# Out by seven products in all four large blocks, with the combined weights made in the plain blocks

## The chip, the cores and the metric

The kernel runs on one core of a Trainium2 chip. The metric is the time of one execution on the device, in microseconds (us). Five engines work side by side, each through its own queue in order: TensorE (PE) multiplies, VectorE (DVE) and ScalarE (ACT) do elementwise work, GpSimd (POOL) helps with attention, and SyncE (SP) issues the DMAs between DRAM and on-chip memory.

## The reference

```python
# attention, q of 8 batches x 8 heads x 576 x 64; k and v averaged over groups of 8 rows (72 rows left)
scores = (1 / sqrt(64)) * q @ k_p.T
attn   = softmax(scores)
x      = (attn @ v_p) arranged as [4608 tokens, 512]
# then a gated layer
h = x @ w_in                       # w_in 512 x 2048
g = h * clip(h + 3, 0, 6) / 6
out = g @ w_out                    # w_out 2048 x 512
```

The weights arrive in 64-bit floats, the rest in 32-bit.

## The kernel before

The 4608 tokens are done in twelve blocks (`BLOCKS`, 512, 256 and ten of 384 tokens). The first four (0 to 3) are "plain"; the other eight are taken in pairs as four "large blocks" of 768 tokens (`supers`, numbered 0 to 3 here). Attention for a later block is cut into small steps that `Paced` spreads over the matmuls of the current one.

Every operand is kept as a high and a low part in the fp32r format, and each product is three matmuls (high x high, high x low, low x high); the stationary operand is always 128 x 128.

A plain block goes through 16 steps, one for each tile of 128 features (`NF`). Step u does `h` (x by w_in, 12 matmuls into one of two PSUM banks, `psh`), then `relu` on ACT, `gate` on DVE, `hi` (tile `ghi`) on ACT and `lo` (tile `glo`) on DVE; `out` (g by w_out into `pso`) comes two steps later. h(u) can begin when gate(u - 2) has read the bank of the same number. The weights stay in SBUF, in tiles `w_f` of the pools `consts[0]` (f below 8) and `consts[1]`. During blocks 2 and 3, functions in a table `hooks` (block, then step) also prepare the large blocks.

A large block multiplies matrices cut in 2 x 2 blocks with seven block products in place of eight. Its in stage (N1, seven products for each of 8 feature pairs) needs x in seven combinations (`x_ops`, run in the plain block 3 for large block 0) and w_in in seven (three raw, four combined). `sums_of` makes the four combined ones: two sums of a pair of tiles and four mixes on DVE, a rounded copy on ACT, a difference on DVE; tile `wq`, stored to DRAM arrays `wd`. `plain_of` stores the raw blocks (to `wd`, and those of w_out to `w2d`).

The out stage has two forms. `out_plain` (large block 0) multiplies g by w_out directly, 288 matmuls of 512 columns. `out_seven` (1 to 3) does seven products of half width, 504 matmuls of 256 columns, with four combined forms of w_out from the DRAM arrays `w2t`. Those are made once, by `combine`, in the out stage of large block 0, where the weights pass by anyway: sums of 512, mixes of 256 and a difference of 1024 elements on DVE (tiles `tq`, `tg`, `th`), a copy of 1024 on ACT, two stores of 512 KB each.

In the large blocks all weights are read back in pieces of 512 KB (`chunk`) into two rings, `ws0` (wsFalse) and `ws1` (wsTrue). The rings lie where the plain blocks' weights were: `swap` frees `consts[0]` in block 3, and the right side is freed after it.

Up to step 3 of block 1 the order of every engine is written out by hand (`ORDER`). From there a scheduler sets each engine's order when the program is built, from its own estimates; on the chip each engine then keeps to that order and waits on semaphores.

Of the kernel before, what the change touches and what calls it, by code (L numbers as in the profile page):

```python
# [98 lines left out]
def attention_moe_kernel(  # L99
# [833 lines left out]
    def sums_of(i, h):  # L933

        half = slice(h * P, (h + 1) * P)
        t = early_x[-1].tile([P, 2, 4, P], F32, name="wq", bufs=1)
        hi, q = t[:, 0], t[:, 1]
        for r, w in enumerate(pair_of(i)):
            nc.vector.tensor_tensor(  # L939
                out=q[:, 2 * r : 2 * r + 2], in0=w[:, 0, :, half], in1=w[:, 1, :, half], op=ALU.add  # L940
            )
            after_mark()
        for to, a, b, how in ((0, 0, 2, ALU.subtract), (2, 2, 3, ALU.add), (3, 3, 0, ALU.subtract), (1, 1, 3, ALU.subtract)):
            nc.vector.tensor_tensor(out=q[:, to], in0=q[:, a], in1=q[:, b], op=how)
# [18 lines left out]
    def chunks_of(n):  # L963
        if n not in SEVEN:
            plain = [w2_dram[f // 4][:, f % 4].rearrange("p q m c -> p (q m c)") for f in range(NF)]
        else:
            plain = []
            for o in KINDS:
                for m in range(NF // 4):
                    if o in RAW2:  # L970
                        r, q = RAW2[o]
                        plain.append(w2_dram[m][:, r::2, q].rearrange("p k m c -> p k (m c)"))
                    else:
                        plain.append(w2t_dram[m][:, PLACED[o]].rearrange("p k m c -> p (k m c)"))
# [31 lines left out]

    def combine(n, i):

        if i % 2 or not i:
            hi, q = (late[1].tile([P, 2 * DM], F32, name=x, tag="ro", bufs=NREL) for x in ("th", "tq"))  # L1010
        else:
            t = late[1].tile([P, 8 * HALF], F32, name="tg", tag=f"g{i - 2}", bufs=1)
            hi, q = t[:, : 2 * DM], t[:, 2 * DM : 4 * DM]
        hi, q = (x.rearrange("p (a c) -> p a c", a=4) for x in (hi, q))
        for r in range(2):
            w = next_w2(n, 2 * i + r).bitcast(F32)
            nc.vector.tensor_tensor(out=q[:, 2 * r : 2 * r + 2], in0=w[:, :, 0], in1=w[:, :, 1], op=ALU.add)
            after_mark()
        for to, a, b, how in ((3, 3, 1, ALU.subtract), (1, 1, 0, ALU.subtract), (0, 0, 3, ALU.add), (2, 2, 0, ALU.subtract)):
            nc.vector.tensor_tensor(out=q[:, to], in0=q[:, a], in1=q[:, b], op=how)  # L1020
            after_mark()
        nc.scalar.copy(hi.bitcast(F32R), q)
# [544 lines left out]
```

## Time and profile before

| | us |
|---|---|
| median of 3 runs | 894.1 (892.81 to 894.3) |
| the profiled execution, its time | 893.88 |
| its span in the profile | 892.1 |
| the four plain blocks, to the start of large block 0 | 345.6 |
| in stage and out stage of large block 0 | 77.6 and 70.8 |
| of large block 1 | 71.6 and 67.2 |
| of large block 2 | 71.2 and 64.7 |
| of large block 3 | 59.5 and 63.9 |

The stages are cut where PE goes over to matmuls of another line. A row of a stretch has, after its length, the busy time and the number of instructions of each engine, the granted TensorE clock, the share of the DMA engines that is busy and GB/s. A row of the chain is one piece of the sequence of work that ended last, with its start, its length and the count of instructions. A row of the timeline has the start, the length and the instruction, and in square brackets the engine's idle time before it and what ended that. Instructions of one engine that follow each other may overlap a little, so start to start is shorter than the length.

### The profile page before, as it was taken

Reading aid. Unit: us, or ns where it says so; the run is one execution under the profiler, and the core shown is the slowest. Engines: PE = TensorE matmul, PEld = TensorE weight load, DVE = VectorE, ACT = ScalarE, POOL = GpSimd, SP = SyncE. Lnnn points to the kernel's source line nnn. Section 1 sums busy time; section 2 is a strip of 40 time slices with the busy share of each in tenths; the row PEclk is TensorE's granted clock in tenths of the full one; section 3 lists DMA queues with packets and bytes.
Section 4 is the critical chain, followed back from the end, with each engine's and each line's share of the span. In section 5 each row is a group of like instructions: output and inputs, shape, how many; then the busy total and the mean of one; then the engine's idle time right before and its main releaser. Section 6 shows DMA issues by size and latency. Waiting matters only on the chain.

```text
span 892.1 us, 15646 instructions
## 1 busy us (share of the span) xinstructions
PE 869.2 (97%) x5360; PEld 812.3 (91%) x5360; DVE 665.9 (75%) x1340; ACT 553.6 (62%) x1515; POOL 83.6 (9%) x168
## 2 busy tenths in 40 slices
PE   7899999999999999999999999999999999999998
PEld 6788888988989998998888999999999999999998
DVE  6999864567877785869788688897597877466664
ACT  5998766655656655778344688665577746355442
POOL 4100002110211100102000101100100200000000
PEclk9999999999999999999999999999999999999999
DMA  9970205995425234996587968877976777877873
GB/s 294 392 293 1 72 24 192 360 327 167 130 67 160 71 129 135 368 315 225 180 271 239 383 218 295 265 239 236 331 250 213 226 233 240 275 253 238 266 264 132
DMA packets 124654, 200.00 MB, mean 224 GB/s; under 512 B 13216, under 2 KB 81056, under 8 KB 124576
## 3 DMA queue, kind: packets, MB, share of 16 engines
q1 hardware_dynamic: 124432, 199.00, 67.8%
q8 instruction: 43, 0.70, 0.3%
q14 instruction: 35, 0.29, 0.1%
q10 hardware_dynamic: 144, 0.00, 0.0%
HBM read 158.08 MB, written 40.89 MB: 223 GB/s over the span
## 4 chain that ended last, share of the span: by engine, by line
PE 80%; DVE 8%; DMA 5%; ACT 4%; issue 2%; SPq 1%; POOL 0%; DVEq 0%; ACTq 0%; POOLq 0%
PE psx L1134 22%; PE psx L1261 19%; PE pso L872 12%; PE psh L841 12%; PE psx L1188 7%; PE psa L646 3%; PE psa L463 3%; ACT e L472 2%; PE psa L572 1%; DMA raw<-w_in_l 1%; DMA raw<-w_out_l 1%; DMA wd<-wq 1%; DVE vst L383 1%; DMA wsFalse<-wd 1%; DVE wq L939 1%
## 5 line engine op out<-in xcount | busy, mean ns | idle before, releaser
L1134 PE MATMUL psx<-x,wsFalse 128*128 128x384 f32 x768 | 151.8, 341 | 1.7 <-DVE g L1098 0.8
L841 PE MATMUL psh<-xhi,w 128*128 128x384 f32 (+2 forms) x520 | 145.9, 340 | 0.5 <-DVE g L853 0.4
L1134 PEld LDWEIGHTS psx<-x,wsFalse 128*128 128x128 f32 x768 | 133.6, 188 | 3.2 <-ACT c L1107 1.3
L1113 ACT CAST part<-g 128x768 fp32r<-128x768 f32 x100 | 83.3, 836 | 85.0 <-PE psx L1261 65.8
L1115 DVE TENSOR_TENSOR part<-g,part 128x768 fp32r<-128x768 f32 x100 | 95.2, 955 | 46.5 <-ACT part L1113 46.1
L872 PE MATMUL pso<-w,ghi 128*128 128x512 f32 x384 | 120.7, 398 | 0.4 <-ACT o L877 0.4
L1134 PE MATMUL psx<-x,wsTrue 128*128 128x384 f32 x576 | 115.8, 342 | 2.4 <-DMA wsTrue<-wd 2.3
L1261 PE MATMUL psx<-wsFalse,part 128*128 128x256 f32 x864 | 108.3, 282 | 1.5 <-DVE part L1115 1.1
L1261 PEld LDWEIGHTS psx<-wsFalse,part 128*128 128x128 f32 x864 | 105.2, 189 | 2.3 <-DVE part L1115 1.3
L1134 PEld LDWEIGHTS psx<-x,wsTrue 128*128 128x128 f32 x576 | 99.6, 188 | 3.1 <-DVE g L1092 3.1
L841 PEld LDWEIGHTS psh<-xhi,w 128*128 128x128 f32 x520 | 93.2, 188 | 8.2 <-DVE g L853 1.1
L472 ACT ACTIVATE e<-psa,mx 128x72 f32<-128x72 f32 x256 | 78.6, 324 | 23.7 <-DVE mx L467 22.4
L841 PE MATMUL psh<-xlo,w 128*128 128x384 f32 (+2 forms) x260 | 87.1, 336 | 0.0
L501 POOL TENSOR_TENSOR a<-e,sm 128x256 f32<-128x256 f32 x60 | 41.0, 683 | 478.3 <-DVE sm L490 377.9
L1261 PE MATMUL psx<-wsTrue,part 128*128 128x256 f32 x648 | 81.3, 283 | 0.0
L1261 PEld LDWEIGHTS psx<-wsTrue,part 128*128 128x128 f32 x648 | 79.3, 191 | 0.2 <-DVE part L1115 0.2
L872 PEld LDWEIGHTS pso<-w,ghi 128*128 128x128 f32 x384 | 69.1, 188 | 11.2 <-ACT o L877 0.7
L1090 ACT ACTIVATE r<-g,small 128x384 f32<-128x384 f32 x96 | 58.8, 621 | 28.4 <-DVE g L1098 28.0
L872 PE MATMUL pso<-w,glo 128*128 128x512 f32 x192 | 74.4, 399 | 0.0
L1098 DVE TENSOR_TENSOR g<-psx,c 128x384 f32<-128x384 f32 x96 | 52.3, 553 | 28.7 <-PE psx L1134 20.6
L1107 ACT COPY c<-psx 128x384 f32<-128x384 f32 x96 | 45.0, 485 | 28.5 <-PE psx L1134 28.1
L1092 DVE SCALAR_TENSOR_TENSOR g<-r,g 128x384 f32<-128x384 f32 x96 | 54.5, 576 | 9.7 <-ACT r L1090 9.2
(139 smaller groups left out, 1473.2 us busy)
## 6 DMA issues: line engine op xcount, KB each, us to landing
wsFalse<-wd SPq DMA_DIRECT2D x64, 512.0 KB, 4.6
wsTrue<-wd SPq DMA_DIRECT2D x48, 512.0 KB, 4.9
wsFalse<-w2d SPq DMA_DIRECT2D x31, 512.0 KB, 5.0
wsFalse<-w2t SPq DMA_DIRECT2D x27, 512.0 KB, 5.0
wsTrue<-w2d SPq DMA_DIRECT2D x21, 512.0 KB, 5.0
wsTrue<-w2t SPq DMA_DIRECT2D x21, 512.0 KB, 4.9
raw<-w_in_l SPq DMA_DIRECT2D x16, 512.0 KB, 8.6
raw<-w_out_l SPq DMA_DIRECT2D x16, 512.0 KB, 9.2
```

Source lines behind the costliest of these rows:

```text
L472: nc.scalar.activation(self.e[:, h], self.ps[:, h], AF.Exp, bias=self.mx[:, h : h + 1], accum_out=self.sm[:, h : h + 1])
L841: nc.tensor.matmul(self.ps, l[f][:, c, :], r[:, c, :], start=c == 0 and i == 0, stop=c == NCC - 1 and i == 2)
L872: nc.tensor.matmul(pos, l, r, start=f == 0 and i == 0, stop=f == NF - 1 and i == 2)
L1090: nc.scalar.activation(r, src, AF.Relu, bias=half_low, scale=GSCALE / (6.0 * WSCALE))
L1092: nc.vector.scalar_tensor_tensor(out=g_of[i][:, k], in0=r, scalar=GSCALE, in1=src, op0=ALU.min, op1=ALU.mult)
L1098: nc.vector.tensor_tensor(out=g_of[i][:, k], in0=ps, in1=kept, op=ALU.add)
L1107: nc.scalar.copy(c, ps)
L1113: nc.scalar.copy(t[:, 0], src)
L1115: nc.vector.tensor_tensor(out=t[:, 1], in0=src, in1=t[:, 0].bitcast(F32), op=ALU.subtract)
L1134: nc.tensor.matmul(ps, w[:, l, c * P : (c + 1) * P], t[:, r, c], start=o in (1, 2, 5) and c == 0 and k == 0, stop=c == 1 and k == 2, skip_ ...
L1188: nc.tensor.matmul(to, l, w[:, qs, r], start=f == 0 and k == 0, stop=end and k == 2)
L1261: nc.tensor.matmul(to, t[:, l, k, i * P : (i + 1) * P], w[:, k, r], start=begin and k == 0 and y == 0 and i % 2 == 0, stop=m == NM - 1 and ...
```

## The change

`out_plain`, `combine` and their tables go; all four large blocks use `out_seven`, now `out_of`. The four combined forms of w_out are made in plain block 3 by the new `sums_of_out`, from the weights in SBUF, each into the place of a weight tile that is no longer needed (`room`). `sums_of` now runs for whole tiles in block 1 (pairs 0 to 2), for half tiles in block 2 (pairs 3 to 6) and once whole in block 3 (pair 7). The tiles of x in block 1 share one place, which leaves room for the sums there. `store` ties each plain store to the PE instruction recorded last, which holds it back in the scheduler's order.

```diff
-SEVEN = (1, 2, 3)
-MAKE = (range(8), (), (), ())
-TURN = (0, 2, 4, 6, 7, 9, 10, 12)
...
+            elif j == 1:
+                t = early_x[-1].tile([P, 2, NCC, max(BLOCKS) // 2], dtype, name="x01", tag="xhi", bufs=1)
+                xs[j, "xhi"], xs[j, "xlo"] = t[:, 0], t[:, 1]
...
+    def sums(blocks, mixes, hi, q):
+        for r, (high, low) in enumerate(blocks):
+            nc.vector.tensor_tensor(out=q[:, 2 * r : 2 * r + 2], in0=high, in1=low, op=ALU.add)
             after_mark()
+        for to, a, b, how in mixes:
             nc.vector.tensor_tensor(out=q[:, to], in0=q[:, a], in1=q[:, b], op=how)
         nc.scalar.copy(hi.bitcast(F32R), q)
         nc.vector.tensor_tensor(out=q.bitcast(F32R), in0=q, in1=hi, op=ALU.subtract)
...
+    def room(f):
+        if f:
+            t = const(f).tile([P, 2, 4, 2 * P], F32, name="wq", tag=f"w_{f}")
+            return t[:, 0], t[:, 1]
+        return (
+            early_x[-1].tile([P, 4, 2 * P], F32, name="wq", bufs=1),
+            const(0).tile([P, 4, 2 * P], F32, name="wq", tag="w_0_0"),
+        )
...
+    def sums_of_out(i, place):
+        hi, q = place()
+        blocks = [w_of[2 * i + r, 1].bitcast(F32).rearrange("p m (q c) -> p m q c", q=2) for r in range(2)]
+        sub, add = ALU.subtract, ALU.add
+        sums([(w[:, 0], w[:, 1]) for w in blocks], ((3, 3, 1, sub), (1, 1, 0, sub), (0, 0, 3, add), (2, 2, 0, sub)), hi, q)
+        for m, t in enumerate((hi, q)):
+            nc.sync.dma_start(w2t_dram[i // 2][:, :, i % 2, m], t)
...
     def store(to, src):
         nc.sync.dma_start(to, src)
+        behind(traced[-1], next(i for i in reversed(traced) if i.engine == mybir.EngineType.PE).name)
...
-        (out_seven if n in SEVEN else out_plain)(n, j, bank, parts, split_g, split_f, pairs, second_att, rest, last_h)
+        out_of(n, j, bank, parts, split_g, pairs, second_att, rest, last_h)
...
-    make = [lambda i=i, h=h: sums_of(i, h) for i in range(NPR) for h in range(2)]
...
+    hooks = {1: {}, 2: {}, 3: {}}
+    for i, u in enumerate((4, 8, 11)):
+        hooks[1][u] = [lambda i=i: sums_of(i, every, lambda: early_room(2 * P, "xlo"))]
+    for n in range(8):
+        hooks[2][2 * n] = [lambda n=n: sums_of(3 + n // 2, halves[n % 2], lambda: early_room(P, "wq"))]
...
+    hooks[3].setdefault(2, []).append(lambda: sums_of(NPR - 1, every, lambda: room(0)))
+    for i, (u, f) in enumerate(((3, 0), (4, 1), (5, 2), (6, 3), (7, 4), (8, 5), (10, 8), (12, 9))):
+        hooks[3].setdefault(u, []).append(lambda i=i, f=f: sums_of_out(i, lambda: room(f)))
```

The order on VectorE in block 3, from the gate of step 8 to the gate of step 9, before (`g` is the gate, `glo` the low part, `ksum` belongs to attention, `wq` to the sums of w_in):

```order
L853 SCALAR_TENSOR_TENSOR g<-g,psh 128x384
L861 TENSOR_TENSOR glo<-g,ghi 128x384
L264 TENSOR_REDUCE ksum<-kst 128x72
L939 TENSOR_TENSOR wq<-w_1096 128x256
L939 TENSOR_TENSOR wq<-w_1150 128x256
L944 TENSOR_TENSOR wq<-wq 128x128 x4
L946 TENSOR_TENSOR wq<-wq 128x512
L853 SCALAR_TENSOR_TENSOR g<-g,psh 128x384
```

And in the changed kernel, between the same two gates:

```order
L850 SCALAR_TENSOR_TENSOR g<-g,psh 128x384
L936 TENSOR_TENSOR wq<-wq 128x256 x5
L858 TENSOR_TENSOR glo<-g,ghi 128x384
L260 TENSOR_REDUCE ksum<-kst 128x72
L936 TENSOR_TENSOR wq<-wq 128x256
L933 TENSOR_TENSOR wq<-w_1006 128x512
L933 TENSOR_TENSOR wq<-w_1049 128x512
L936 TENSOR_TENSOR wq<-wq 128x256 x2
L938 TENSOR_TENSOR wq<-wq 128x1024
L850 SCALAR_TENSOR_TENSOR g<-g,psh 128x384
```

Mixes of 256 and differences of 1024 elements, of several combinations in turn, now stand between one gate and the next; they were of 128 and 512.

The order on SyncE around the end of block 3, before (`wd<-wq` stores of sums, `out<-o` results of block 3, `ws` loads for large block 0):

```order
L948 DMA wd_118<-wq 128x2x128
L948 DMA wd_117<-wq 128x2x128 x2
L878 DMA out<-o 128x512
L948 DMA wd_119<-wq 128x2x128
L948 DMA wd_118<-wq 128x2x128
L948 DMA wd_117<-wq 128x2x128 x2
L878 DMA out<-o 128x512 x2
L992 DMA wsFalse<-wd_99 128x1024
L992 DMA wsTrue<-wd_96 128x1024
L992 DMA wsTrue<-wd_97 128x1024
```

And in the changed kernel (`w2t<-wq` are the stores of the combinations):

```order
L967 DMA w2t_126<-wq 512x1x256 x3
L1013 DMA wsFalse<-wd_92 128x1024
L1013 DMA wsFalse<-wd_93 128x1024
L1013 DMA wsFalse<-wd_94 128x1024
L1013 DMA wsFalse<-wd_95 128x1024
L967 DMA w2t_127<-wq 512x1x256 x4
L1013 DMA wsTrue<-wd_96 128x1024
L875 DMA out<-o 128x512 x3
L1013 DMA wsTrue<-wd_97 128x1024
```

The first wsTrue load now stands behind the last four stores of combinations and ahead of block 3's results.

More of the change, by code (lines that the diff above doesn't have):

```diff
@@ L45 @@
 RAW2 = {1: (0, 0), 2: (1, 0), 3: (1, 1)}
-SEVEN = (1, 2, 3)
-MAKE = (range(8), (), (), ())
-TURN = (0, 2, 4, 6, 7, 9, 10, 12)
 CUTS = (.85, 0.85, 0.85, 0)
-TAIL = 5
 WSCALE = 2.0**8
@@ L608, in x_tile @@
                 xs[j, name] = pool.tile([P, NCC, TMAX], dtype, name=name, bufs=2)
-            else:
-                xs[j, name] = early_x[-1].tile(
-                    [P, NCC, max(BLOCKS) if j < 2 else TMAX], dtype, name=name, bufs=1
-                )
+            elif j == 1:
+                t = early_x[-1].tile([P, 2, NCC, max(BLOCKS) // 2], dtype, name="x01", tag="xhi", bufs=1)
+                xs[j, "xhi"], xs[j, "xlo"] = t[:, 0], t[:, 1]
+            else:
+                xs[j, name] = early_x[-1].tile([P, NCC, TMAX if j else BLOCKS[0]], dtype, name=name, bufs=1)
         return xs[j, name][:, :, : BLOCKS[j]]
@@ L961, in plain_of, with chunks_of @@
                 store(w2_dram[f // 4][:, f % 4, :, m], w)
[L963 to L974, printed above, removed]
+    def chunks_of():
+        plain = []
+        for o in KINDS:
+            for m in range(NF // 4):
+                if o in RAW2:
+                    r, q = RAW2[o]
+                    plain.append(w2_dram[m][:, r::2, q].rearrange("p k m c -> p k (m c)"))
+                else:
+                    plain.append(w2t_dram[m][:, PLACED[o]].rearrange("p k m c -> p (k m c)"))
         return [w.rearrange("p k m c -> p (k m c)") for w in w_dram] + plain
@@ L997, in attention_moe_kernel @@
         first_of.append(len(chunks))
-        chunks += chunks_of(n)
+        chunks += chunks_of()
     def next_w(n, m):
@@ L1005, in next_w2 @@
         return chunk(first_of[n] + len(w_dram) + x).rearrange("p (k m c) -> p k m c", k=2, m=2)
[L1007 to L1022, printed above, removed]
-        nc.vector.tensor_tensor(out=q.bitcast(F32R), in0=q, in1=hi, op=ALU.subtract)
-        after_mark()
-        for m, x in enumerate((hi, q)):
-            nc.sync.dma_start(w2t_dram[i // 2][:, :, i % 2, m], x)
     x_op = {}
@@ L1117, in split_g @@
             parts[key] = t
-        def split_f(f):
-            split_g(f, g_of[f // 2][:, f % 2 :: 2])
         for m, (i, o) in enumerate(N1):
@@ L1204, in out_seven, with out_of @@
-    def out_seven(n, j, bank, parts, split_g, split_f, pairs, att, rest, last_h):
+    def out_of(n, j, bank, parts, split_g, pairs, att, rest, last_h):
         NT2, NM, W2 = HALF // P, NF // 4, DM // 2
```

69 lines of the change are left out of this document (12 added, 57 removed).

## Prediction

> **What bounds the kernel now.** I read the page first, then the stretches (cut where the shape of the PE instructions changes), then the chain, then the timelines where the change puts its work.
>
> ```profile
> PE 869.2 (97%) x5360; PEld 812.3 (91%) x5360; DVE 665.9 (75%) x1340; ACT 553.6 (62%) x1515; POOL 83.6 (9%) x168
> PE 80%; DVE 8%; DMA 5%; ACT 4%; issue 2%; SPq 1%; POOL 0%; DVEq 0%; ACTq 0%; POOLq 0%
> ```
>
> PE is busy almost always and carries 80% of the chain, so PE work that goes counts in full, unless another engine then needs longer than PE in some stage. By stretch (start:end, length, then busy us and count of PE, PEld, DVE, ACT, POOL):
>
> ```profile
> 126.00:186.00 60.00, 60.00 (x387) 54.54 (x386) 35.54 (x98) 40.46 (x154) 11.99 (x24) 1.00 0.74 246
> 186.00:266.00 80.00, 77.69 (x418) 69.62 (x417) 58.91 (x158) 45.40 (x158) 11.04 (x20) 1.00 0.55 162
> 266.00:345.60 79.60, 79.60 (x430) 72.61 (x429) 60.61 (x146) 46.50 (x140) 7.11 (x14) 1.00 0.38 111
> 423.20:494.00 70.80, 70.80 (x328) 58.38 (x327) 58.04 (x99) 30.47 (x50) 1.97 (x4) 1.00 0.74 237
> 565.60:632.80 67.20, 65.92 (x538) 65.14 (x538) 52.66 (x79) 36.58 (x69) 2.05 (x5) 1.00 0.78 251
> 704.00:768.70 64.70, 64.49 (x532) 64.30 (x531) 47.22 (x61) 32.33 (x50) 1.18 (x2) 1.00 0.77 248
> ```
>
> These are plain blocks 1, 2 and 3, and the out stages of large blocks 0 (plain), 1 and 2 (by seven). VectorE has 19.0 us to spare in block 3 (79.6 - 60.6) and 24.5 in block 1. The granted clock is 1.00 throughout.
>
> **Out by seven in large block 0.** PE's pace, start to start, from pieces of the chain (start, length, count):
>
> ```profile
> 333.25 2.08 PE pso L872 x9
> 335.34 2.10 PE psh L841 x12
> ...
> 464.96 28.36 PE psx L1188 x123
> ...
> 828.34 59.47 PE psx L1261 x498
> ```
>
> A 512-column matmul takes 28.36/123 = 0.231, a 256-column one 59.47/498 = 0.119 and a 384-column one 2.10/12 = 0.175 us. Removed: 16 feature tiles x 6 token tiles x 3 parts = 288, x 0.231 = 66.4. Added: 7 products x 3 token tiles x 8 feature tiles x 3 parts = 504, x 0.119 = 60.2. PE loses 6.2 us of work. By the stages it is 70.8 - 67.2 = 3.6 to 70.8 - 64.7 = 6.1, since each also holds some attention and the start of a by-seven stage waits for its first splits. I take -5.2. The 28 weight loads instead of 16 fit a stage that already runs so at a DMA share of 0.77.
>
> **The out weights are combined in block 3.** Eight combinations leave large block 0 and enter block 3 (one a step, u = 3 to 8, 10, 12), in place of eight half sums of w_in, of which one whole sum stays. VectorE's prices, by group (min/median/max ns) and then back to back (start, duration):
>
> ```profile
> L1020 DVE TENSOR_TENSOR tq<-tq x20: 417/419/429, 428.9 to 486.2; 128x256 f32<-128x256 f32 x20
> L1017 DVE TENSOR_TENSOR tq<-wsFalse x8: 683/685/693, 427.4 to 480.1; 128x512 f32<-128x512 f32 x8
> L1022 ACT CAST th<-tq x5: 1047/1048/1055, 431.1 to 486.7; 128x1024 fp32r<-128x1024 f32 x5
> L1023 DVE TENSOR_TENSOR tq<-tq,th x5: 1219/1225/1226, 432.2 to 487.8; 128x1024 fp32r<-128x1024 f32 x5
> ```
>
> ```profile
> 454.03 1.29 DVE L1017 TENSOR_TENSOR tg<-wsFalse 128x512 f32<-128x512 f32 x2
> 455.24 0.42 DVE L1020 TENSOR_TENSOR tq<-tq 128x256 f32<-128x256 f32 x1
> 455.57 0.42 DVE L1020 TENSOR_TENSOR tg<-tg 128x256 f32<-128x256 f32 x1
> ...
> 460.79 1.22 DVE L1023 TENSOR_TENSOR tg<-tg 128x1024 fp32r<-128x1024 f32 x1
> 461.93 0.95 DVE L1115 TENSOR_TENSOR part<-g,part 128x768 fp32r<-128x768 f32 x1
> ```
>
> ```profile
> 304.24 0.75 DVE L264 TENSOR_REDUCE ksum<-kst 128x72 f32<-128x576 f32 x1
> 304.91 0.28 DVE L944 TENSOR_TENSOR wq<-wq 128x128 f32<-128x128 f32 x1
> ...
> 319.48 2.69 DVE L1038 TENSOR_TENSOR x<-x,x 128x768 fp32r<-128x768 f32 x3
> 322.09 0.96 DVE L1046 TENSOR_TENSOR x<-x,mid 128x768 f32<-128x768 f32 x1
> ...
> 328.90 0.56 DVE L853 SCALAR_TENSOR_TENSOR g<-g,psh 128x384 f32<-128x384 f32 x1
> 329.37 0.94 DVE L944 TENSOR_TENSOR wq<-wq 128x128 f32<-128x128 f32 x3
> ...
> 342.34 0.55 DVE L853 SCALAR_TENSOR_TENSOR g<-g,psh 128x384 f32<-128x384 f32 x1 [0.79 <-ACT g L849]
> 343.47 0.56 DVE L861 TENSOR_TENSOR glo<-g,ghi 128x384 fp32r<-128x384 f32 x1 [0.58 <-ACT ghi L857]
> ```
>
> Start to start, a 512-element sum takes 1.21/2 = 0.605, a mix of 256 0.335, a difference of 1024 1.14, an x operation 2.61/3 = 0.87, a ksum 0.67, a gate or glo 0.47. A combination is 2 x 0.605 + 4 x 0.335 + 1.14 = 3.7 us. The total of block 3 would still fit (60.6 - 8 half sums + 9 x 3.7 stays under 79.6), but VectorE is served in order, and the order of the new kernel bunches the work: little up to step 5, nearly all of it from step 6 on. Counted there, from the gate of step 6 to the last glo of step 15: 32 mixes 10.7, 14 sums 8.5, 8 differences 9.1, 11 x operations 9.6, 10 gates and 10 glo 9.4, 4 ksum 2.7, and 5 small ones of attention, 1.4 at most at the pace of a mix: 51.4 us. PE, from the end of step 6's h to the end of step 15's out: 108 x 0.231 + 136 x 0.175 + nine short ones, some 1.0 = 49.7 us. The queue cannot overlap its ends with PE: the first gate starts some 1.3 after its h (a relu on ScalarE, then the hand-over), and after the last glo comes some 1.4 of out. I add 2.0 for differences that find their ScalarE cast (1.05) not ready. 51.4 + 1.3 + 1.4 + 2.0 - 49.7 = +6.4 us. PE waits for it where h(u) needs the PSUM bank that gate(u - 2) frees, and behind step 12, where the x operations stand. The low end, no cast waited for and ends of 1.0 and 0.7, is +3.4. At full durations (0.42, 0.685, 1.22, 0.955, 0.555, 0.75 and some 0.35 each) instead of start-to-start times the sum is 59.2 and the high end +14.2. I take the start-to-start times, because the two rows of 0.42 begin 0.33 apart.
>
> [...]
>
> **The start of large block 0.** PE's row and the chain:
>
> ```profile
> 349.87 6.50 PE L1134 MATMUL psx<-x,wsFalse 128*128 128x384 f32 x36
> 358.70 1.47 PE L1134 MATMUL psx<-x,wsTrue 128*128 128x384 f32 x7 [2.34 <-DMA wsTrue<-wd]
> ...
> 353.22 5.34 DMA wsTrue<-wd
> ```
>
> PE waits 2.34 us for the first wsTrue load, which takes 5.34. The late half sums that held SP's queue there are gone, but now the load stands behind four stores of combinations, the last of which waits for VectorE's difference some 3 us before step 15's out ends. PE has 18 wsFalse products, 3.2 us, before it asks. Issue 1.2 and landing 5.3 after -3 give 3.5: a wait of 0.3 to 1.3. I take -1.0, ends -2.3 and +2.
>
> **Blocks 1 and 2.** Three whole sums of w_in go into block 1: 3 x 3.7 = 11.1 us of VectorE, 35.5 + 11.1 of 60, so PE covers them; if a bunch delays a gate, PE loses a part of one sum. Block 2 keeps eight half sums. I take +0.5 (ends -1 and +3). The plain stores of block 1 move into blocks 2 and 3, where the DMA share is 0.55 and 0.38; 16 stores of combinations of 512 KB add some 105 GB/s to block 3's 111. Nothing on PE waits for them, unless an x tile reuses a weight's place whose store has not landed: then VectorE, already the late engine, waits, and its gates with it.
>
> **Sum.** The profiled execution took 893.88 us (span 892.1; the median of the runs is 894.1). 893.88 - 5.2 + 6.4 - 1.0 + 0.5 = 894.6.
>
> **Rivals.** (1) VectorE in block 3 costs much more than 6.4: the full durations, since many of its instructions wait on a semaphore, or x operations that wait for stores. For it: the high end +14.2; against it: the overlapping rows. With +10 to +14.2 the time is 898 to 902. This is slower from a term of about +7.5 up. (2) VectorE's bunch is mostly absorbed: PE has two h banks and three glo buffers of slack, and earlier gates make the queue enter step 6 without a backlog. With +3.4, -6.2 and -2.0 the time is 889.6; it is faster wherever the term stays below about 3.7. For it: 19.0 us to spare in block 3, all PE-bound before. Against it: the bunch is in an order that cannot change at run time. (3) The out stage gains only 3.6, because its start waits for the first splits as in large block 1: 896.2 with all else as forecast.
>
> **Chances.** A measurement of this kernel tells some 0.2%, 1.8 us, from no change. The forecast, in which block 3 takes back what out gains, has 0.35 (892.1 to 895.9). Rival 2 has 0.32. Rivals 1 and 3, both slower, have 0.24 and 0.09. The range 889.5 to 901.0 takes in rival 2 at its price and rival 1 up to nearly its high end.
>
> **What would show it.** In the new profile's stretches the out stage of large block 0 should take about 65.6 instead of 70.8; block 3 should be some 6 longer, with DVE above 0.9 of its second half, PE's idle time there ending on DVE g or glo, and the chain running through wq. If block 3 shows no PE wait, rival 2 is right. If VectorE's rows there start a full duration apart, or wait for landings, rival 1 is. The forecast fails if PE's pace in large block 0 is not the 0.119 of the last.

## The result: slower by 1.2%

| | before | after |
|---|---|---|
| median, four runs each (lowest to highest), us | 893.45 (891.7 to 894.3) | 904.04 (901.35 to 905.75) |
| the profiled execution, time and span | 893.88, 892.1 | 905.75, 904.0 |

After over before is 1.0118, 95% interval 1.0087 to 1.015. The forecast was 894.6 with a range up to 901.0.

The page of the changed kernel, busy time of the engines and shares of the chain that ended last:

```profile
PE 869.7 (96%) x5576; PEld 821.8 (91%) x5576; DVE 686.7 (76%) x1345; ACT 565.3 (63%) x1528; POOL 82.6 (9%) x168
PE 71%; DVE 12%; DMA 7%; SPq 4%; ACT 3%; issue 2%; DVEq 0%; ACTq 0%
```

TensorE is as busy as before (869.7 against 869.2 us), though it has less to multiply, and its part of the chain fell from 80% to 71%: waits came in. Where, the stretches tell (start:end, length, busy us and count of PE, PEld, DVE, ACT and POOL, granted clock, DMA share, GB/s). They are block 1, block 2, block 3, and the in stage and the out stage of large block 0:

```profile
126.10:189.80 63.70, 62.34 (x401) 55.80 (x399) 47.05 (x122) 44.57 (x171) 13.91 (x27) 1.00 0.44 135
189.80:270.00 80.20, 78.54 (x421) 70.69 (x421) 56.74 (x155) 43.61 (x143) 8.30 (x17) 1.00 0.59 179
270.00:358.00 88.00, 78.70 (x402) 69.30 (x402) 74.79 (x153) 50.39 (x133) 7.00 (x14) 0.98 0.74 244
358.00:440.30 82.30, 77.46 (x445) 75.53 (x444) 67.05 (x158) 60.64 (x202) 11.87 (x24) 0.96 0.83 281
440.30:506.90 66.60, 66.40 (x556) 66.20 (x555) 48.42 (x69) 34.93 (x71) 2.71 (x6) 1.00 0.73 237
```

Cut at the same matmuls, the kernel before has block 3 (76.4 us) and the in stage here:

```profile
269.10:345.60 76.50, 76.50 (x411) 69.94 (x411) 57.71 (x138) 45.09 (x137) 7.11 (x14) 1.00 0.39 116
345.60:423.20 77.60, 73.95 (x441) 72.08 (x440) 59.55 (x151) 58.71 (x200) 11.94 (x24) 1.00 0.86 288
```

So the out stage gained 4.2 (70.8 to 66.6), as meant; block 3 lost 11.5 (76.4 to 87.9), the in stage of large block 0 lost 4.7 (77.6 to 82.3), what lies ahead of block 3 lost 0.9, and large block 1 gave 1.3 back (71.6 to 70.7 and 67.2 to 66.8). That makes +11.6 of the span's +11.9.

The cut between block 3 and the in stage is the first product of large block 0. In the kernel before, 9 `out` matmuls of block 3 still stand behind it, in the changed kernel 18. Nine take 2.1 us, so block 3's own loss is 2.1 larger than 11.5, and the in stage's is 2.1 smaller than 4.7. The two together, 154.0 before and 170.2 after, do not depend on the cut.

**Block 3.** VectorE's timeline at 301 to 307 and at the end of the block (start, length, instruction, and in brackets the idle time before it and what ended it):

```profile
301.31 0.42 DVE L581 TENSOR_TENSOR alo<-psa,ahi 128x256 fp32r<-128x256 f32 x1 [0.44 <-ACT ahi L579]
305.26 1.29 DVE L933 TENSOR_TENSOR wq<-w 128x512 f32<-128x512 f32 x2 [3.52 <-DMA wd<-wq]
306.59 0.28 DVE L594 TENSOR_TENSOR arem<-psa,arem 32x128 fp32r<-32x128 f32 x1
306.90 0.55 DVE L850 SCALAR_TENSOR_TENSOR g<-g,psh 128x384 f32<-128x384 f32 x1
...
360.51 0.56 DVE L858 TENSOR_TENSOR glo<-g,ghi 128x384 fp32r<-128x384 f32 x1 [0.58 <-ACT ghi L854]
```

The row at 305.26 is the first sum of combination 0. Its place (`room(0)`) is the one in which the sums of pair 7 were made, and VectorE waits 3.52 us until their stores have landed; the gate of step 6 stands behind it. These sums end with a difference at 295.58, and SyncE issues their eight stores right after it:

```profile
295.58 1.29 DVE L938 TENSOR_TENSOR wq<-wq 128x1024 fp32r<-128x1024 f32 x1 [0.23 <-ACT wq L937]
297.44 5.24 SPq L958 DMA_DIRECT2D wd<-wq  x8
```

From the gate at 306.90 to the end of the last glo VectorE runs nearly without a pause, 54.2 us. TensorE, at the end of the block, and the stretches around it:

```profile
352.22 0.69 PE L838 MATMUL psh<-xhi,w 128*128 128x384 f32 x1 [3.31 <-DVE g L850]
```

```profile
348.80:352.10 3.30, 0.11 (x1) 0.00 (x0) 3.30 (x6) 0.83 (x1) 0.00 (x0) 1.00 1.04 379
352.10:355.60 3.50, 3.38 (x11) 3.38 (x12) 3.50 (x7) 1.81 (x3) 0.00 (x0) 0.51 0.05 17
434.00:440.80 6.80, 6.00 (x22) 6.03 (x23) 6.45 (x21) 4.80 (x19) 0.98 (x2) 0.50 0.48 147
```

TensorE stands idle for 3.31 us, and in the 3.5 us behind that its granted clock is 0.51. Such stretches of half clock stand at 352.1 (3.41 us) and 434.0 (6.83 us); the kernel before has none.

**The in stage of large block 0.** VectorE first, then TensorE:

```profile
430.26 0.69 DVE L379 TENSOR_TENSOR vst<-vst 96x512 f32<-96x512 f32 x1 [2.64 <-DMA vst<-vr_l]
430.87 0.55 DVE L1092 SCALAR_TENSOR_TENSOR g<-r,g 128x384 f32<-128x384 f32 x1
431.34 0.55 DVE L1098 TENSOR_TENSOR g<-psx,c 128x384 f32<-128x384 f32 x1
```

```profile
431.94 1.32 PE L1131 MATMUL psx<-x,wsTrue 128*128 128x384 f32 x6 [2.87 <-DVE g L1098]
434.80 0.66 PE L568 MATMUL psa<-ident,a 128*128 128x128 f32 x2 [1.54 <-ACT e L468]
435.32 2.27 PE L1131 MATMUL psx<-x,wsTrue 128*128 128x384 f32 x6
```

One addition for attention waits for a load; two gates stand behind it, and TensorE waits for them. Then six matmuls take 2.27 us, which take 1.32 at full clock.

### The profile page after: what moved, and what is told of

Its sections match the earlier page's. It is cut to its first block, busy times and chain, and to the rows that moved or that the text cites. A ratio compares the mean times of both kernels' runs of the same rounds, so it can differ in the third digit from the quotient of the medians.

```text
span 904.0 us, 16200 instructions
## 1 busy us (share of the span) xinstructions
PE 869.7 (96%) x5576; PEld 821.8 (91%) x5576; DVE 686.7 (76%) x1345; ACT 565.3 (63%) x1528; POOL 82.6 (9%) x168
## 4 chain that ended last, share of the span: by engine, by line
PE 71%; DVE 12%; DMA 7%; SPq 4%; ACT 3%; issue 2%; DVEq 0%; ACTq 0%
PE psx L1214 25%; PE psx L1131 23%; PE psh L838 8%; PE pso L869 7%; PE psa L459 3%; PE psa L643 3%; SPq L958 2%; DVE wq L933 1%; DMA wd<-wq 1%; DVE wq L936 1%; DMA kst<-k_l 1%; DVE wq L938 1%; SPq L974 1%; PE psa L568 1%; DMA vst<-vr_l 1%
## 5 line engine op out<-in xcount | busy, mean ns | idle before, releaser
L1113 ACT CAST part<-g 128x768 fp32r<-128x768 f32 x112 | 93.7, 837 | 88.5 <-PE psx L1214 86.5
L1115 DVE TENSOR_TENSOR part<-g,part 128x768 fp32r<-128x768 f32 x112 | 106.6, 955 | 53.2 <-ACT part L1113 52.9
L1214 PE MATMUL psx<-wsFalse,part 128*128 128x256 f32 x1152 | 143.9, 282 | 0.0
L1214 PEld LDWEIGHTS psx<-wsFalse,part 128*128 128x128 f32 x1152 | 140.3, 189 | 0.0
L838 PE MATMUL psh<-xhi,w 128*128 128x384 f32 (+2 forms) x392 | 121.3, 362 | 7.9 <-DVE g L850 7.3
L869 PE MATMUL pso<-w,ghi 128*128 128x512 f32 x384 | 117.3, 398 | 0.0
L1214 PE MATMUL psx<-wsTrue,part 128*128 128x256 f32 x864 | 110.5, 283 | 1.7 <-DVE part L1115 1.1
L1214 PEld LDWEIGHTS psx<-wsTrue,part 128*128 128x128 f32 x864 | 106.4, 191 | 2.7 <-ACT kept L1189 1.4
L838 PEld LDWEIGHTS psh<-xhi,w 128*128 128x128 f32 x392 | 73.1, 190 | 16.1 <-DVE g L850 8.8
L468 ACT ACTIVATE e<-psa,mx 128x72 f32<-128x72 f32 x256 | 78.8, 326 | 13.1 <-DVE mx L463 11.2
L838 PE MATMUL psh<-xlo,w 128*128 128x384 f32 (+2 forms) x196 | 70.0, 357 | 0.7 <-DVE xlo L622 0.7
```

The lines of the kernel that those rows point to most:

```text
L468: nc.scalar.activation(self.e[:, h], self.ps[:, h], AF.Exp, bias=self.mx[:, h : h + 1], accum_out=self.sm[:, h : h + 1])
L838: nc.tensor.matmul(self.ps, l[f][:, c, :], r[:, c, :], start=c == 0 and i == 0, stop=c == NCC - 1 and i == 2)
L869: nc.tensor.matmul(pos, l, r, start=f == 0 and i == 0, stop=f == NF - 1 and i == 2)
L1113: nc.scalar.copy(t[:, 0], src)
L1115: nc.vector.tensor_tensor(out=t[:, 1], in0=src, in1=t[:, 0].bitcast(F32), op=ALU.subtract)
L1214: nc.tensor.matmul(to, t[:, l, k, i * P : (i + 1) * P], w[:, k, r], start=begin and k == 0 and y == 0 and i % 2 == 0, stop=m == NM - 1 and ...
```

## The experiments

Each kernel ran beside the kernel before on the same chip; its median there was 893.45 to 895.35. Lengths of stages are cut where TensorE goes over to matmuls of another line. Every time and ratio, and the stages that moved (block 3 ends at the first product of large block 0):

| run | median | ratio to before (95%) | block 1 | block 2 | block 3 | in, large block 0 | out |
|---|---|---|---|---|---|---|---|
| before | | 1 | 60.1 | 83.0 | 76.4 | 77.6 | 70.8 |
| after | 904.04 | 1.0118 (1.0087, 1.015) | 63.7 | 80.3 | 87.9 | 82.3 | 66.6 |
| e1 no pacing | 924.86 | 1.0334 (1.0307, 1.0361) | 72.6 | 94.4 | 86.6 | 79.3 | 66.3 |
| e2 no combining | 898.35 | 1.0049 (1.003, 1.0067) | 72.9 | 77.0 | 77.8 | 80.4 | 66.4 |
| e3 pair 7 early | 897.81 | 1.0033 (1.0021, 1.0046) | 63.7 | 79.3 | 85.5 | 79.2 | 65.9 |
| e4 before, paced | 905.98 | 1.0122 (1.0097, 1.0147) | 61.6 | 77.6 | 80.2 | 89.7 | 71.1 |
| e5 no combining, fixed order | 891.64 | 0.9971 (0.9956, 0.9985) | 63.7 | 81.1 | 75.9 | 81.2 | 66.3 |
| e6 one add later | 899.17 | 1.0057 (1.0042, 1.0072) | 63.7 | 80.4 | 87.9 | 77.6 | 66.3 |
| e7 gap filled | 902.10 | 1.0092 (1.0077, 1.0107) | 63.7 | 79.6 | 85.7 | 81.4 | 66.4 |
| e8 spread | 910.10 | 1.0187 (1.0164, 1.021) | 63.7 | 79.2 | 99.6 | 76.5 | 64.9 |
| e9 mixes on GpSimd | 906.74 | 1.013 (1.011, 1.0151) | 63.7 | 80.2 | 92.0 | 81.4 | 66.5 |
| e10 e3 and e9 | 900.67 | 1.0063 (1.0047, 1.0079) | 63.7 | 78.7 | 85.9 | 82.7 | 66.3 |
| e11 own place | 895.69 | 1.002 (1.0005, 1.0035) | 63.7 | 79.3 | 79.8 | 81.7 | 68.3 |
| e12 four in block 1 | 899.87 | 1.0074 (1.0051, 1.0096) | 69.8 | 76.8 | 80.7 | 81.5 | 66.3 |
| e13 both causes | 891.09 | 0.9969 (0.9956, 0.9982) | 63.7 | 79.6 | 79.7 | 78.4 | 66.8 |
| e14 gates first | 894.07 | 1.0001 (0.9989, 1.0012) | 63.7 | 81.9 | 75.8 | 84.5 | 66.8 |
| e15 tail in order | 893.62 | 0.9995 (0.9982, 1.0008) | 63.7 | 78.7 | 75.9 | 84.8 | 66.8 |

Behind the first product of large block 0 stand 9 `out` matmuls of block 3 in the kernel before, e2 and e4, none in e8 and 18 in the others.

### First round: pacing, combining, pair 7

e1, no pacing:

```diff
     def store(to, src):
         nc.sync.dma_start(to, src)
-        behind(traced[-1], next(i for i in reversed(traced) if i.engine == mybir.EngineType.PE).name)
```

> The changed kernel with the pacing of the plain stores taken out (the extra order edge in store). Theory B (the bunch: VectorE's 54 us of combinations, relu gates and residuals in the second half of block 3 are too much, wherever their stores stand): SyncE's queue is no part of it, block 3 stays within 1.5 us of its 86.0 and the time within 2 of 904. Theory Q (the queue: the eight stores of the sums of pair 7 stand behind paced plain stores, so that VectorE waits 3.5 us at 301.7, and the late vst loads are behind them too): the wait of 3.5 goes, the waits of TensorE at 348 and the halved clock behind it with it, and the time is 897 to 900. Theory C (pacing keeps the queue free for the loads of q, k and ws): without it blocks 2 and 3 wait for loads, 906 to 912.

Block 3 stays (86.6; the 86.0 of the expectation is the 87.9 of the table, counted from a later matmul), as theory B says. Theory Q falls by the row at 297.44 above: the eight stores of pair 7 are issued from 0.6 us after their difference ends, so no plain store holds them back in SyncE's queue; VectorE waits while the eight are issued (5.24 us) and land. None of the three theories has the time, for 22.6 us are lost ahead of block 3. TensorE's waits from 185 to 222 us (total, times, longest):

```profile
PE psh L838 <- DVE xlo L622: 15.6, 1, 15.6
```

Block 2's x is split late: the last whole sum of block 1 lies in the place of `xlo`, and its stores stand behind plain stores. So, in the order that the scheduler makes, the pacing belongs to the change. It is no wait on the chip: the edge only sets where the scheduler puts a store.

e2, no combining:

```diff
     def sums_of_out(i, place):
-        hi, q = place()
-        ...
+        for r in range(2):
+            w = w_of[2 * i + r, 1].bitcast(F32).rearrange("p m (q c) -> p m q c", q=2)
+            for m in range(2):
+                nc.sync.dma_start(w2t_dram[i // 2][:, 2 * r : 2 * r + 2, i % 2, m], w[:, m])
```

> The changed kernel without the arithmetic of the out weights' combinations: sums_of_out stores the weights themselves (four stores a pair where there were two), so VectorE and ScalarE do none of them and the out stages multiply wrong weights of the same size. Theory B: block 3 goes from 86.0 us to 74 to 76, the halved clock of 3.4 us at 352 is gone, and the time falls by 9 to 12, to 892 to 895. Theory Q: the wait of 3.5 for the stores of pair 7 no longer stops anything either, so this kernel alone cannot tell Q's part from B's; the stores now number 32 instead of 16, and if SyncE's queue is what hurts, vst still comes late in large block 0 (a TensorE wait of 2.9 and a half clock of 6.8 at 434 stay). With both, 892 to 898.

Block 3 fell to 77.8, but block 1 grew from 63.7 to 72.9, where nothing was edited: the scheduler ordered the whole program anew. The time, 898.35, above theory B's 892 to 895, is no measure of the combining alone; e5 repeats it in a fixed order.

e3, the sums of pair 7 in block 2:

```diff
-    for n in range(8):
-        hooks[2][2 * n] = [lambda n=n: sums_of(3 + n // 2, ...)]
+    for n, u in enumerate((0, 2, 3, 5, 6, 8, 9, 11, 12, 14)):
+        hooks[2][u] = [lambda n=n: sums_of(3 + n // 2, ...)]
-    hooks[3].setdefault(2, []).append(lambda: sums_of(NPR - 1, every, lambda: room(0)))
```

> The changed kernel with the sums of pair 7 taken out of block 3: ten half sums in block 2 in place of eight, nothing at step 2 of block 3. Theory B: block 3 loses about 5 us of VectorE's work and the wait of 3.5 in front of it, so it shrinks by 6 to 9; block 2 grows by 0 to 2; the time is 896 to 900. Theory Q: the combinations' own stores still stand behind paced plain stores, so a wait for a store of a combination's place is not removed, only that of the shared place: 899 to 901. If block 2 has no room for two more half sums (its VectorE is 0.8 busy), block 3 starts later by 2 to 4 and the gain is under 4: 900 to 902.

6.2 us faster than the changed kernel, and inside theory B's 896 to 900, but not by its mechanism: block 3 fell only by 2.4, not by 6 to 9. The last two half sums were made at 282 and 293 us, in block 3 after all, the first of them behind a wait of 2.0 for stores. The combinations then began at 291.7, 23.5 us after the block's start, without a wait. More came from stages that were not edited, such as the in stage (82.3 to 79.2).

e4, the kernel before with the pacing added to its `store`:

> The kernel before with only the pacing added to its plain stores. Theory B: no change, 892.5 to 895. Theory Q: the half sums of pairs 4 to 7 in block 3 share one place, so each waits for four stores behind paced plain stores; block 3 grows by 2 to 5 and the time is 896 to 899. Theory C (pacing helps the loads): 890 to 892.

It took 905.98, ratio 1.0122 (1.0097, 1.0147). Block 3 grew by 3.8, as theory Q says, but block 2 became 5.4 shorter, and large block 0 began 1.3 earlier than in the kernel before. The loss is not where Q looks for it: the in stage of large block 0 grew from 77.6 to 89.7, with a wait of 3.95 us for a wsTrue load, two of 2.5 and 2.7 and 10.2 us of half clock. So a changed order of the queues alone can cost as much as the whole change did, and runs that let the scheduler order anew say little about one part.

### Second round: the changed kernel's order, with one thing altered

For e5 to e7 each engine's order was read from the changed kernel and written down: every instruction is tied behind the one before it on its engine (`behind`), so nothing else moves.

e5, the arithmetic of the combinations left out (the 16 stores write raw weights):

```diff
     def sums_of_out(i, place):
-        hi, q = place()
-        ...
+        for m in range(2):
+            w = w_of[2 * i + m, 1].bitcast(F32).rearrange("p m (q c) -> p (m q) c", q=2)
+            nc.sync.dma_start(w2t_dram[i // 2][:, :, i % 2, m], w)
```

> The changed kernel with every engine's order written down as it stands there, and only the combinations' arithmetic left out: 56 operations of VectorE and 8 casts of ScalarE are gone, the 16 stores stay where they stand and write the weights themselves. (In e2 the scheduler had made another order of the whole rest, and block 2 began 8 us later.) Theory B: block 3 goes from 87.9 us to 77 to 78, all that comes before it stays within 0.5, the stretch after it too, and the time falls by 10 to 11, to 893 to 894. If much of block 3's excess is the order of what is left (SyncE's queue, the sums of pair 7, the x operations), block 3 stays above 80 and the time above 896.

Block 3, the stretch of it:

```profile
269.40:345.40 76.00, 75.66 (x401) 68.27 (x402) 46.99 (x98) 42.71 (x126) 7.02 (x14) 1.00 0.91 300
```

TensorE has no pause left, VectorE has 47.0 us of work in place of 74.8, and the time is 12.4 us lower. The stores, now without arithmetic ahead of them, hold nothing up, at 300 GB/s in this stretch. Theory B is shown: the combinations' work on VectorE and ScalarE, with what waits around it, costs 12.0 us of block 3 (87.9 to 75.9). Block 3 and the in stage together are 157.1, so 13.1 of the 16.2 us that they had lost are back.

e6, one VectorE instruction moved in large block 0:

```diff
 alo   L581 128x2x128
-vst   L379 96x512
 g     L1092 128x384
 g     L1098 128x384
 vst   L379 128x512
 arem  L594 32x128
 mx    L463 128x4
+vst   L379 96x512
```

> The changed kernel in its own order, with one VectorE instruction moved: in the in stage of large block 0 the first vst add of 96x512, which waited 2.64 us for a load of vr_l while two gates and two small operations of attention stood behind it, goes behind those four. Theory O (an in-order queue blocked by one wait, and the halved clock that follows TensorE's idle time): the waits of 2.9 and 1.5 at 429 to 435 and the 6.8 us of half clock at 434 go or shrink, the stage of 82.3 us falls by 4 to 7, the time to 897 to 900. Rival: the vst rows are needed by the matmuls right behind, so the wait only moves on: 902 to 904.

```profile
428.10 0.55 DVE L1098 TENSOR_TENSOR g<-psx,c 128x384 f32<-128x384 f32 x1
428.57 0.68 DVE L379 TENSOR_TENSOR vst<-vst 128x512 f32<-128x512 f32 x1
429.27 0.28 DVE L594 TENSOR_TENSOR arem<-psa,arem 32x128 fp32r<-32x128 f32 x1
429.59 0.46 DVE L463 TENSOR_REDUCE mx<-psa 128x4 f32<-128x288 f32 x1
430.19 1.14 DVE L379 TENSOR_TENSOR vst<-vst 96x512 f32<-96x512 f32 x2
```

The addition comes as early as it did and nothing waits behind it. The half clock is gone, the stage is 4.7 shorter (77.6), the time 4.9 us lower. What this stage lost besides block 3's matmuls was one instruction's place in a queue.

e7, matmuls in TensorE's pause:

```diff
+    def fill():
+        to = psum.tile([P, 512], F32, name="fill", tag="o3")
+        for k in range(12):
+            nc.tensor.matmul(to, w_in_hi[NF - 1][:, k % NCC, :], w_out_hi[NF - 1], start=True, stop=True)
```

> The changed kernel in its own order, with 12 matmuls of 128x512 into an unused bank put in front of the last h of block 3, where TensorE stood idle for 3.3 us. They compute nothing that is used. Theory H (idle time of TensorE halves its clock for a stretch of 3.4 us): the clock stays at 1.0 there, and h and out behind it take half the time of the 3.4 us, so large block 0 begins 1.5 to 1.8 us earlier although TensorE does 2.8 us more work: 902 to 902.6. Rival (the lower clock comes from something else, a power limit or a fixed schedule): it stays, the work comes on top or fits the gap: 904 to 905.

```profile
347.63 2.90 PE L1465 MATMUL fill<-w,w 128*128 128x512 f32 x12
351.11 0.44 PE L838 MATMUL psh<-xhi,w 128*128 128x384 f32 x1 [0.58 <-DVE g L850]
```

```profile
352.20:355.70 3.50, 3.39 (x18) 2.65 (x16) 3.50 (x8) 1.50 (x3) 0.00 (x0) 1.00 0.00 0
```

The clock stays at 1.00, 18 matmuls pass where 11 did, block 3 is 2.2 us shorter, the time 1.9 lower, with more work on TensorE. Theory H is shown. Not all of the 2.2 is the clock, though. From the start of the last h to the first product of large block 0 it is 4.54 us (351.11 to 355.65) where it was 5.77 (352.22 to 357.99), 1.2 less. The other 1.0 was there before the fill: in this execution the wait for the stores of pair 7 was 2.49 us, not 3.52.

```profile
304.14 1.29 DVE L933 TENSOR_TENSOR wq<-w 128x512 f32<-128x512 f32 x2 [2.49 <-DMA wd<-wq]
```

With the same order on VectorE, the gate of step 6 and the last glo both come 1.0 earlier in the block (35.8 for 36.9, 90.0 for 91.0). So in this order the wait goes through to the end of the block in full.

### Third round: where the bunch begins

e8, e9, e10 and e12 tried to take work out of block 3. In all five runs of this round the scheduler ordered the rest anew, so e4's warning holds for them. e8 makes 14 half pieces in block 2 (pairs 3 to 7, and the combinations of pairs 6 and 7) and six combinations in block 3:

> A version with the same work spread: the sums of pair 7 and the combinations of pairs 6 and 7 are made as halves in block 2 (14 half pieces there in place of 8), and block 3 makes six combinations in place of eight and the pair. Theory B: block 3 has some 14 us less of VectorE's work than in the changed kernel and 9 less than in e3, so it falls from 87.9 to 76 to 79 us; block 2, where VectorE was 0.65 busy, grows by 0 to 2; the rest as in e3: 886 to 891, faster than the kernel before. Rival: block 2's one small place makes each half wait for the stores of the last, VectorE's queue is blocked and block 2 grows by 4 or more: 892 to 897.

910.1, ratio 1.0187 (1.0164, 1.021), outside both ranges. Block 3's own work is some 12 us shorter, which is theory B's side: its last out ends 80.2 after its start, in the changed kernel 94.3 with 2.1 of large block 0's products in between. What the rival says of the one place is seen too, but later than it was put: block 2 did not grow (79.2), and the loss stands at the end of block 3. VectorE's waits in blocks 2 and 3 and TensorE's row behind them:

```profile
DVE wq L933 <- DMA wd<-wq: 14.6, 8, 3.8
```

```profile
365.80 1.32 PE L459 MATMUL psa<-kbd,qt 128*128 128x144 f32 x4 [14.99 <-DMA qt<-q_l]
```

The half pieces, which share one place, begin 9 to 13 us apart in block 2 (at 197.0, 208.4, 221.7, 232.1 and so on), so 14 do not fit into its 79 us. The last is made at 348, and SyncE's queue holds its stores in front of the q loads of large block 0. From 280 to 347 us TensorE had no wait.

e9 gives the 32 mixes of the combinations to GpSimd, e10 the same with e3:

```diff
-            nc.vector.tensor_tensor(out=q[:, to], in0=q[:, a], in1=q[:, b], op=how)
+            (mixer or nc.vector).tensor_tensor(out=q[:, to], in0=q[:, a], in1=q[:, b], op=how)  # nc.gpsimd in sums_of_out
```

> The changed kernel with the 32 mixes of 128x256 of the out weights' combinations on GpSimd in place of VectorE, nothing else; the scheduler orders the rest anew. VectorE loses 32 x 0.335 = 10.7 us of its 54 in the second half of block 3; GpSimd, 0.05 busy there, gets 32 x some 0.68 (its 128x256 product of attention) = 22. Theory B (it is VectorE's bunch that counts, not the stores nor ScalarE): block 3 falls from 87.9 to 79 to 82 and the time to 895 to 899. Rival (a combination's latency counts, since each place is used once and the mixes on GpSimd take twice as long and two hand-overs more; or the two engines slow each other): block 3 stays above 85, the time 901 or more.

> The same with the sums of pair 7 made in block 2, as in e3 (897.8). Theory B: block 3 from 85.5 to 76 to 79, and its two halved clocks of 3.4 us are gone: 887 to 892, at or below the kernel before. Rival as for e9: 895 to 899.

906.74 and 900.67, ratios 1.013 (1.011, 1.0151) and 1.0063 (1.0047, 1.0079). e9 is no faster than the changed kernel and its block 3 is longer, 92.0 to 87.9; e10 is slower than e3, with block 3 at 85.9 to 85.5 (and above the rival's 895 to 899). The rival holds: 32 instructions of 0.42 us each (12.7 us busy) left VectorE, and nothing was gained. Groups of VectorE in 270 to 362 us (count, busy, mean ns, idle before), the changed kernel's and then e9's, and GpSimd's in e9:

```profile
L933 DVE TENSOR_TENSOR wq<-w 128x512 f32<-128x512 f32 x18 | 12.1, 714 | 3.5 <-DMA wd<-wq 3.5
L858 DVE TENSOR_TENSOR glo<-g,ghi 128x384 fp32r<-128x384 f32 x17 | 9.4, 553 | 1.3 <-ACT ghi L854 1.3
L850 DVE SCALAR_TENSOR_TENSOR g<-g,psh 128x384 f32<-128x384 f32 x17 | 9.3, 549 | 2.5 <-ACT g L846 2.4
```

```profile
L933 DVE TENSOR_TENSOR wq<-w 128x512 f32<-128x512 f32 x18 | 15.4, 896 | 4.0 <-DMA wd<-wq 4.0
L858 DVE TENSOR_TENSOR glo<-g,ghi 128x384 fp32r<-128x384 f32 x16 | 11.2, 703 | 2.0 <-ACT ghi L854 2.0
L850 DVE SCALAR_TENSOR_TENSOR g<-g,psh 128x384 f32<-128x384 f32 x15 | 8.2, 549 | 3.2 <-ACT g L846 3.1
```

```profile
L936 POOL TENSOR_TENSOR wq<-wq 128x256 f32<-128x256 f32 x32 | 34.5, 1093 | 21.0 <-DVE wq L933 20.0
L497 POOL TENSOR_TENSOR a<-e,sm 128x256 f32<-128x256 f32 x6 | 4.1, 679 | 33.2 <-DVE sm L486 33.2
```

A mix took 1.09 us on GpSimd where 0.68 was expected, and VectorE's operations with two inputs in SBUF went from 0.714 to 0.896 and from 0.553 to 0.703, while the gate, which reads one input from PSUM, stayed at 0.549. What slowed the others was not shown.

e12 makes four whole sums in block 1 (steps 3, 5, 8, 11) and none in block 3:

> The changed kernel with four whole sums in block 1 (pairs 0 to 3, at steps 3, 5, 8 and 11) in place of three, eight half sums of pairs 4 to 7 in block 2, and nothing but the eight combinations in block 3. Theory B with W: against e3 (block 3 85.5) two half sums, 5 us of VectorE, leave block 3 too, and the combinations start some 8 us earlier; block 3 is 79 to 82, block 1 as it was (63.7), and the time 889 to 894. Rival (block 1's one place takes 12 to 16 us a sum, so the fourth makes block 2 begin later by 2 to 4): 893 to 897.

899.87, ratio 1.0074 (1.0051, 1.0096). Block 3 came to 80.7, as expected. But block 1 grew from 63.7 to 69.8, of which 3.1 were left when block 3 began (271.3, in e3 268.2): that is the rival's price. The in stage, at 81.5 with 6.8 us of half clock, took the rest of what is over the rival's 893 to 897.

e11 leaves the work in block 3 and changes the places, and with them the steps of pair 7 and of six combinations:

```diff
-    hooks[3].setdefault(2, []).append(lambda: sums_of(NPR - 1, every, lambda: room(0)))
-    ... ((3, 0), (4, 1), (5, 2), (6, 3), (7, 4), (8, 5), (10, 8), (12, 9))
+    hooks[3].setdefault(5, []).append(lambda: sums_of(NPR - 1, every, lambda: room(2)))
+    ... ((3, 0), (4, 1), (6, 3), (7, 4), (8, 5), (10, 8), (11, 9), (13, 10))
```

> The changed kernel, where the sums of pair 7 no longer share a place with the first combination: combinations 0 and 1 come first, into w_0 and w_1, the sums of pair 7 follow at step 5 into w_2, and the other six combinations each take the place after (w_3, w_4, w_5, w_8, w_9, w_10). The same work, and no store to wait for in front of the bunch. Theory W (the 3.5 us that VectorE waited at 301.7 for the stores of pair 7 push everything behind by as much, since VectorE is not idle again until block 3 ends, and the last gate's wait, with the halved clock, is the sum of it): block 3 falls from 87.9 by 3.5 to 5 and the time to 899 to 901. Rival: the wait took the place of another one (its inputs, a busy ScalarE) or the later places, which come free only from step 10 on, set the end: block 3 within 1.5 of 87.9, 903 to 905.

```profile
289.51 1.29 DVE L933 TENSOR_TENSOR wq<-w 128x512 f32<-128x512 f32 x2
```

```profile
268.20:348.00 79.80, 76.04 (x401) 68.12 (x401) 72.22 (x149) 48.12 (x132) 6.94 (x14) 1.00 0.79 262
```

Combination 0 begins at 289.5, 21.3 us after the block's start (in the changed kernel at 305.3, 35.3 after), without a wait. Block 3 is 8.1 us shorter, more than expected, with the same work. The wait is gone, and the gate of step 6 comes 3.8 earlier in the block (33.1 for 36.9), which is theory W's 3.5. The rest of the 8.1 is more than theory W: the bunch moved forward into time in which VectorE had been half idle, the order is another, and the halved clock moved behind the block's end (it begins at 348.5, in the in stage, which has 81.7). What each of these is worth was not separated. An early beginning alone is not enough: in e3 combination 0 began 23.5 after the block's start without a wait, but the gate of step 6 came only 36.5 after, and block 3 took 85.5.

### Fourth round: the two causes together

e13 is e11 in its own order with the addition of e6 moved:

> The kernel of e11 (the sums of pair 7 in a place of their own) in its own order, with the vst add of 96x512 that waited 1.79 us at 423.0 behind the seven instructions that follow it. If the late place and the blocked queue are two causes that add up, the in stage of large block 0 falls from 81.7 to 77 to 78.5, the out stage from 68.3 to 66.5, and the time from 895.7 to 889 to 891, below the kernel before by some 0.4%. If the wait only moves on (in e11 the two arem and alo operations behind it are also late), 893 to 896.

```profile
347.50:425.90 78.40, 76.76 (x443) 74.19 (x444) 65.24 (x151) 59.57 (x195) 12.07 (x22) 0.98 0.89 297
425.90:492.70 66.80, 66.57 (x557) 66.17 (x556) 52.36 (x81) 37.10 (x79) 4.34 (x8) 1.00 0.74 241
```

The two add up, 4.9 (e6) and 8.4 (e11) to 13.0: 891.09 against 894.5 for the kernel before, ratio 0.9969 (0.9956, 0.9982). This is the fastest version that leaves nothing out, with the same instructions as the change as made.

e14 puts the last gates and residuals of block 3 ahead of the x operations and combinations that stood before them; e15 mends the new wait that e14 shows:

> The same, and the last three gates and residuals of block 3 in VectorE's queue (with their ScalarE casts) put ahead of x operations and combinations that stood before them. VectorE does the same work there. Theory B in its in-order form (what costs is not that VectorE is full but that a full queue serves the gates last): TensorE's waits of 1.7 and 1.75 us at 340 and 346 and the halved clock of 3.4 us at 348 go, 4 to 5 us: 884.5 to 887. Rival (the amount counts: what was put behind is then waited for by large block 0's first products): 888 to 890.

> The kernel of e14 with its new stall taken out: in e14 ScalarE's copies of the finished sums (o<-pso) stood behind the cast of the last combination and behind the exponentials, which waited for VectorE's last combination, so that TensorE stood idle for 6.0 us at 352 and ran at half clock for 6.8. Here mx and the exponentials come earlier, the copies next, and the cast and the difference of the last combination behind them. Theory B in its in-order form: block 3 stays at 76, the in stage of large block 0 falls from 84.5 to 77 to 79 and the time to 886 to 888.5, 0.7 to 0.9% below the kernel before. Rival (the amount of VectorE's work comes back somewhere else): 890 to 892, no better than e13.

TensorE's rows, of e14 and of e15:

```profile
358.54 2.29 PE L1131 MATMUL psx<-x,wsFalse 128*128 128x384 f32 x6 [6.04 <-ACT o L874]
```

```profile
359.83 2.29 PE L1131 MATMUL psx<-x,wsTrue 128*128 128x384 f32 x6 [4.10 <-DMA wsTrue<-wd]
```

In both, block 3 has no TensorE wait for a gate left (75.8 and 75.9, as without combinations), and the in stage gives more than all of it back (84.5 and 84.8 in place of 78.4): the two together are 160.4 and 160.6, in e13 158.1. In e14 ScalarE's copies of the sums stand behind a cast that waits for the last combination. In e15 those are early, but the wsTrue load, which stands in SyncE's queue behind the last combination's store, is issued at 354.5 and lands 5.3 later. Theory B's in-order form fails in both, and both times, 894.07 and 893.62, lie even above the rival's ranges. What the rival says is seen, that work put behind is waited for elsewhere. But the new waits are again places in a queue, ScalarE's in e14 and SyncE's in e15, so it is not shown that the amount of VectorE's work is the limit. An order with the wsTrue load ahead of the last store, or another one, was not tried.

## Why the prediction was wrong, step by step

**Out by seven, -5.2: right in kind.** It measured -4.2 (-4.5 in e5 and e6), about midway between the forecast and rival 3's 3.6. The stage began with 0.6 us of half clock.

**Block 3, +6.4: this step failed; it measured +11.5, and 2.1 more to its last out.** The forecast was 1.3 (h to first gate) + 53.4 (VectorE's bunch) + 1.4 (end) - 49.7 (TensorE). In the profile the h of step 6 begins 29.3 after the block's start and ends at 301.8, the gate follows at 306.90, the last glo ends at 361.1, and the last out at 364.2: 5.1 + 54.2 + 3.1 - 49.7 = 12.7, twice the forecast. That VectorE would be the late engine was right, and so was the place, behind the x operations: TensorE's 3.31 us end on the gate of step 13, which stands behind them. The bunch itself was sized rightly, by start-to-start times (54.2 for 53.4).

What the sum had wrong are the two ends of the bunch. Its beginning was 3.8 late, by the wait of 3.52 for the stores of pair 7. Its end was 1.7 longer: six products of large block 0 (1.0) stand in TensorE's order between the last glo and the last out, and this out takes 2.1, not 1.4. The text looked for a place whose store has not landed among the x tiles (rival 1), and said of combination 0 only that it is made at step 3; that `room(0)` also holds the sums of pair 7 stands in the diff. e7 shows that such a wait reaches the end of the block in full; e11, without it but in another order, has +3.4, the forecast's low end.

**The start of large block 0, -1.0: inside its ends, but not as priced.** The wait for wsTrue (2.34 before) is gone, 0.4 for another is left: -1.9. The load was issued late, at 360.10, behind the last stores, as forecast; but block 3 was late too, and TensorE asked for it only at 368.3. In e15, where block 3 ends early, the wait is 4.10. **The in stage as a whole, +4.7, was not in the sum:** the forecast took the rest of the stage as it stood. The 2.1 of block 3's matmuls that it now holds and the 1.9 gained at its start nearly cancel. The rest is order, since the scheduler orders anew all that follows an edit: e6 shows 4.7 of it in one instruction.

**Blocks 1 and 2, +0.5:** +0.9, within its ends, but as the sum of +3.6 and -2.7. TensorE has 13 more matmuls of attention in block 1 and 13 fewer in block 2, which the forecast did not foresee.

**The clock** was read as 1.00 throughout, as something given. Behind the pause of 3.31, near the end of the bunch, it costs 1.2 (e7) to 1.7 us (an estimate, half of 3.41), and, with 6.8 us at half rate, by the same estimate about 3.4 of e6's 4.9.

**The rivals.** Rival 1 had the side and nearly the time (898 to 902), and of its two mechanisms the wait for a landing, at another tile; not the full durations. Rival 2 is not e13, though its 889.6 is near e13's 891.1: there block 3 and the in stage together are 4.1 longer than before (rival 2: 3.4 - 2.0 = 1.4), and out gains 4.0, not 6.2. That the totals are near is luck. (By the sum, the border below which rival 2 is faster is 3.9, not 3.7.)

## What to carry to other kernels

When a change lets a step reuse a buffer, list for each place who wrote it last and when that store lands; a wait in front of a full in-order queue moves everything behind it (e7: 1.0 us less of it, and the last glo 1.0 earlier). Where a scheduler makes the order, an edit moves work that it does not touch: compare parts of a change in a fixed order, and read the new order for instructions that wait for a load in front of others that are waited for. Work moved off an engine's critical stage is only gained if the stage that receives it has that time free at that moment, not on the average.
